# Attention with two shared pairs of PSUM banks, and key preparation in one step with the low parts made by TensorE and ScalarE

## The chip, the cores and the metric

The kernel runs on one core of a Trainium2 chip. The metric is the device time in microseconds (us) of one execution. The engines are named as the profile names them: PE (TensorE, matrix products and transposes into PSUM), DVE (VectorE), ACT (ScalarE), POOL (GpSimd) and SP (SyncE, which issues most transfers). PSUM has eight banks of 128 partitions x 512 float32 values.

## What is computed

The reference has three parts, one behind the other:

```
# attention: q, k, v are (4, 8, 576, 64)
scores = (q @ k.T) / 8
scores = where(scores >= max(scores, -1) - tau, scores, -1e9)
attn   = exp(scores - max);  attn = attn / (sum(attn, -1) + 1e-9)
x      = (attn @ v), heads side by side          # 2304 tokens x 512
# first feed-forward part
xn = x / sqrt(mean(x*x) + 1e-6) * rms_g
x  = (silu(xn @ w_gate) * (xn @ w_val)) @ w_out  # 1536 wide
# second feed-forward part
h  = x @ w_in;  out = (h * cos(h)) @ w_out       # 2048 wide
```

## The kernel before

**Precision.** A float32 product is made of "fp32r" products: each operand is split into a high part (`hi`, the value rounded to that form) and a low part (`lo`, what is left), and three products hi x hi, hi x lo and lo x hi are summed in PSUM. So whatever enters a score product needs a hi and a lo part.

**Tiling of the attention.** The work is 16 pairs of heads (two heads of one batch element). A pair has 576 query rows per head, cut into five units: units 0 to 3 hold 128 rows of both heads, unit 4 the last 64 rows of each head. For a pair the kernel loads q, k and v in their natural layout, transposes q and k on PE, and keeps them as hi and lo tiles in SBUF (`qhi`, `qlo` 128 x 512, `khi`, `klo` 128 x 896: the 576 keys with the last 64 of them a second time, and the last 64 queries). This is the **preparation**, three steps for each pair: "b" (512 key columns), "a" (512 query columns) and "c" (384 more key columns, the last queries among them). Each has a step on PE (`prep_pe`, transposes of 128 x 128), one on ACT (`prep_act`, the hi part, for q multiplied by the scale) and one on DVE (`prep_lo`, PSUM value minus hi part).

**A unit of scores.** `s_mm` makes both heads' scores, 576 columns each, in the bank pairs `s0` and `s1`. DVE's `s_max` copies them to SBUF, negated and scaled, with the row minimum (one instruction per head, 144 in all). For units 0 to 3 the factor is the constant 1.0, since q carries the scale, and for unit 4 the column `qscale`. POOL adds the threshold (`s_thr`), ACT takes the exponential (`s_exp`), and DVE multiplies by the mask and sums the rows (`s_mask`, 144). `t_pe` transposes the result on PE in halves of 64 rows into a PSUM tile `pst`, `t_raw` (ACT) copies it out in two halves, `c_pe` and `c_raw` do the last key columns (`psc`). `av` multiplies by v (20 products into `po`), `av_out` (ACT) copies it out, and POOL divides by the row sums (`av_div`), squares and adds for the norm.

**PSUM before.** Scores have `s0` and `s1`, two banks each. `ps_t` is one bank for the preparation, `psc`, the norm's sums and the fillers; `ps_h` two banks for `pst`; `ps_v` one bank for `po`. Each of the three holds one tile at a time. `px_open`, which opens the first sums of the feed-forward part, takes all three.

**Clock fillers.** `warm` makes products of a constant that nobody reads: ten before the first data, and three after each of the first six units of scores (`WARM_S`), each as two instructions in the trace.

**What sets the order.** The whole program is a list of steps, and class `Plan` lays it out before anything is built: each step has an engine, a duration and a place from the table `STEPS`, the steps it comes after, the buffers that it takes and frees. Again and again the planner picks the step that could start first by these figures (a smaller place wins a tie; `SWITCH` is added on PE where the tiling of the array changes by the table `TILING`; steps named in `LOCK` do not overlap), and writes its instructions. Every engine then works through its own list in that order, and waits where data or a buffer is not there. So a new table of durations and places changes the order everywhere, in the feed-forward parts too. These are two parts of some 820 us in which PE makes 384- and 512-column products; the first eight pieces of them (`gv_mm`, `px_mm`) follow the attention directly.

Of the kernel before, what the change touches and what calls it, by code (L numbers as in the profile page):

```python
# [18 lines left out]
P = 128  # L19
# [9 lines left out]
    "xl3": ("SP", 2500, 3512077, 4000),  # L29
    "yl": ("SP", 3000, 4063563, 3000),  # L30
    "oc0": ("ACT", 482, 1205589),
    "none": ("", 0, -131642),
    "load_k": ("SP", 1700, -358397, 5000),
    "load_q": ("SP", 2300, 2983338, 7000),
    "load_v": ("SP", 1700, 8925207, 5000),
    "pb": ("PE", 440, 3173980),
    "pa": ("PE", 440, 4428866),
    "pc": ("PE", 355, 3941429),
    "pb_a": ("ACT", 467, 6657236),
    "pa_a": ("ACT", 580, 7839742),  # L40
    "pc_a": ("ACT", 360, 2523842),
    "pa_l": ("DVE", 658, 2612355),
    "pb_l": ("DVE", 603, 2495294),
    "pc_l": ("DVE", 470, -3198829),
    "s": ("PE", 884, -3471316),
    "s4": ("PE", 790, 8623278),
    "warm": ("PE", 640, 4878694),
    "max": ("DVE", 678, -148277),
    "exp": ("ACT", 668, 9896803),
    "th": ("POOL", 300, 4051053),  # L50
    "mask": ("DVE", 737, 2741949),
    "t": ("PE", 480, 3967233),
    "t4": ("PE", 250, 3540467),
    "raw": ("ACT", 467, 3428201),
    "raw4": ("ACT", 280, 1719867),
    "c0": ("PE", 245, 4792815),
    "c1": ("PE", 465, 402678),
    "c_raw": ("ACT", 264, 8087658),
    "radd": ("POOL", 250, 5843718),
    "rinv": ("DVE", 420, 3365343),  # L60
    "r_out": ("SP", 2100, 143277, 2500),
    "r_in": ("SP", 1700, 8607246, 11000),
    "av0": ("PE", 2214, 5385146),
    "av1": ("PE", 2748, 4772949),
    "avo": ("ACT", 345, 4838887),
    "div": ("POOL", 1391, 4284936),
    "xout": ("SP", 800, 8555192, 2500),
    "sq": ("POOL", 1124, 5898793),
    "x_add": ("POOL", 1389, 4440748),
    "xsum": ("PE", 1085, 4834622),  # L70
    "mean": ("DVE", 110, -2375958),
    "rms": ("POOL", 1520, 7212247),
    "rs_out": ("SP", 2500, 5265071, 2500),
    "x_load": ("SP", 600, 836615, 4500),
    "x_p": ("POOL", 980, -1347804),
    "x_a": ("ACT", 507, 2440769),
    "x_d": ("DVE", 500, 3806148),
# [218 lines left out]
def attention_moe_cos_kernel(  # L296
# [31 lines left out]
    def f(ap):  # L328
        return ap.bitcast(F32)
# [1796 lines left out]
```

## Time and profile before

| what | value |
|---|---|
| time, median of 3 runs | 1127.99 us (1122.11, 1127.99, 1129.1) |
| the profiled execution's own time | 1124.89 us |
| its span, first to last instruction | 1123.1 us |
| busy share: PE, PEld, DVE, ACT, POOL | 97%, 86%, 78%, 62%, 39% |
| mean granted clock of PE | 0.985 of full speed |
| first and last score maximum on DVE | 12.2 and 284.1 us |
| last product of the attention (`po`) | starts at 298.3 us |

The attention takes the first 300 us, the two feed-forward parts the rest. Busy time counts an instruction from its start to its end, and on an engine that overlaps neighbours (PE above all, DVE and ACT by a few tens of ns) the distance from one start to the next says what an instruction really costs. PE's clock has two levels here, 2.4 GHz (granted 1.0) and 1.2 GHz (granted 0.5).

### The profile page before, as it was taken

What the parts mean: (1) busy time and instruction counts of PE and PEld (TensorE: products, weight loads), DVE (VectorE), ACT (ScalarE), POOL (GpSimd) and SP (SyncE); (2) the same over time, 40 slices, a digit from 0 to 9 for tenths busy, and PEclk for the clock granted to TensorE, in tenths of its full rate; (3) what the DMA queues carried; (4) which work ended last, traced back from release to release, by engine and by line L of the source; (5) the groups of instructions that cost most, each with busy time, mean ns of one, the idle gap of its engine ahead of it and who ended that gap; (6) DMA issues with size and microseconds to landing.
All of it is one profiled execution on the core that took longest, in us unless ns stands there. A gap on an engine that the chain in (4) does not pass through costs nothing.

```text
span 1123.1 us, 19997 instructions
## 1 busy us (share of the span) xinstructions
PE 1084.1 (97%) x7296; PEld 965.8 (86%) x7296; DVE 876.7 (78%) x1683; ACT 693.0 (62%) x1332; POOL 439.3 (39%) x445
## 2 busy tenths in 40 slices
PE   8889999989899999999999999999999999999998
PEld 7666766766799999999999999998888888889887
DVE  4899999899679777778776664598889988865665
ACT  3788888888556555455544443477667676666553
POOL 1143443524622456465421531345554555132221
PEclk6899999999999999999999999999999999999999
DMA  4244342422344455634313285534444453084533
GB/s 107 75 112 134 88 126 77 110 66 68 114 133 169 141 209 193 229 142 132 94 57 114 89 274 173 192 117 153 167 159 155 152 180 124 1 274 167 171 120 94
DMA packets 113458, 153.04 MB, mean 136 GB/s; under 512 B 51632, under 2 KB 82128, under 8 KB 113360
## 3 DMA queue, kind: packets, MB, share of 16 engines
q1 hardware_dynamic: 112000, 151.31, 41.8%
q8 instruction: 57, 0.93, 0.3%
q10 hardware_dynamic: 1264, 0.43, 0.1%
q14 instruction: 41, 0.34, 0.1%
q0 software_dynamic: 96, 0.03, 0.0%
HBM read 103.16 MB, written 48.58 MB: 135 GB/s over the span
## 4 chain that ended last, share of the span: by engine, by line
PE 61%; DVE 16%; ACT 7%; POOL 6%; DMA 5%; issue 4%; SPq 0%; POOLq 0%; DVEq 0%; ACTq 0%
PE pc L840 24%; PE po L840 12%; PE px L840 8%; PE po L733 5%; PE s L600 5%; PE pst L695 2%; DVE s L621 2%; DVE e L650 2%; POOL wtmp L1086 2%; ACT et L706 2%; DMA raw<-in_moe_w_val_dram 2%; POOL wtmp L1168 2%; DMA raw<-in_moe_w_out_dram 1%; PE pgv L840 1%; DMA raw<-in_moe_w_in_dram 1%
## 5 line engine op out<-in xcount | busy, mean ns | idle before, releaser
L840 PE MATMUL pc<-xh,w 128*128 128x384 f32 x896 | 257.2, 338 | 0.9 <-DVE r L1441 0.9
L840 PEld LDWEIGHTS pc<-xh,w 128*128 128x128 f32 x896 | 164.6, 188 | 3.4 <-DVE r L1441 1.2
L840 PE MATMUL pc<-xl,w 128*128 128x384 f32 x448 | 151.1, 337 | 0.0
L1086 POOL TENSOR_TENSOR wtmp<-wtmp,raw 128x512 int32<-128x512 int32 x68 | 90.4, 1336 | 121.9 <-issue 28.4
L840 PE MATMUL pc<-th,w 128*128 128x384 f32 x448 | 134.3, 340 | 2.3 <-ACT r L1445 1.7
L1685 POOL TENSOR_TENSOR h<-hh,h 128x384 fp32r<-128x384 f32 x64 | 66.3, 1041 | 118.1 <-ACT h L1673 47.8
L840 PE MATMUL po<-w,h 128*128 128x512 f32 x405 | 110.0, 397 | 0.2 <-DVE w L1124 0.2
L1441 DVE TENSOR_TENSOR r<-r,pc 128x384 f32<-128x384 f32 x96 | 52.5, 551 | 69.4 <-ACT r L1445 50.6
L650 DVE SCALAR_TENSOR_TENSOR e<-s,th,e 128x576 f32<-128x576 f32 x128 | 103.5, 841 | 0.9 <-POOL th L631 0.9
L1782 DVE TENSOR_TENSOR acc<-acc,po 128x512 f32<-128x512 f32 x126 | 84.6, 682 | 23.9 <-PE po L840 23.4
L840 PE MATMUL px<-h,w 128*128 128x384 f32 x516 | 102.5, 338 | 0.0
L640 ACT ACTIVATE e<-s,m 128x576 f32<-128x576 f32 x128 | 95.4, 790 | 7.9 <-DVE s L621 7.9
L621 DVE TENSOR_SCALAR_CACHE_REDUCE s<-s 128x576 f32<-128x576 f32 x128 | 91.9, 752 | 10.2 <-PE s L600 10.0
L1445 ACT COPY r<-pc 128x384 f32<-128x384 f32 x96 | 45.7, 479 | 84.5 <-PE pc L840 84.2
L706 ACT COPY et<-pst 128x512 f32<-128x512 f32 (+1 forms) x160 | 80.2, 550 | 27.3 <-PE pst L695 27.0
L840 PEld LDWEIGHTS px<-h,w 128*128 128x128 f32 x516 | 91.7, 188 | 0.0
L840 PEld LDWEIGHTS pc<-th,w 128*128 128x128 f32 x448 | 82.5, 188 | 8.1 <-ACT r L1445 3.1
L840 PEld LDWEIGHTS po<-w,h 128*128 128x128 f32 x405 | 75.3, 188 | 15.2 <-DVE w L1124 0.6
L840 PEld LDWEIGHTS pc<-xl,w 128*128 128x128 f32 x448 | 84.2, 188 | 2.0
L1456 POOL TENSOR_TENSOR h<-q,h 128x384 fp32r<-128x384 f32 x43 | 44.7, 1046 | 83.9 <-DVE q L1484 52.4
L840 PE MATMUL pc<-tl,w 128*128 128x384 f32 x224 | 75.6, 337 | 0.0
L631 POOL TENSOR_SCALAR th<-m,tau_c 128x4 f32<-128x4 f32 (+1 forms) x48 | 30.6, 638 | 111.0 <-DVE s L621 110.2
(194 smaller groups left out, 2717.3 us busy)
## 6 DMA issues: line engine op xcount, KB each, us to landing
wd<-w SPq DMA_DIRECT2D x67, 512.0 KB
w<-wd SPq DMA_DIRECT2D x53, 512.0 KB
raw<-in_moe_w_out_dram SPq DMA_DIRECT2D x30, 512.0 KB
raw<-in_moe_w_in_dram SPq DMA_DIRECT2D x16, 512.0 KB
raw<-in_moe_w_gate_dram SPq DMA_DIRECT2D x14, 512.0 KB
raw<-in_moe_w_val_dram SPq DMA_DIRECT2D x14, 512.0 KB
wq<-wd SPq DMA_DIRECT2D x14, 512.0 KB
x<-xb SPq DMA_DIRECT2D x16, 288.0 KB
```

The costliest lines, as they stand in the source:

```text
L600: nc.tensor.matmul(un[n]["ps", hd][:, c, 0:288], lhs, kh[bb][r, k0:k0 + 288], start=c not in [d for d, _ in todo[:x]], stop=c not in [d fo ...
L621: nc.vector.tensor_scalar(s.rearrange("p (c n) -> p c n", c=2), un[n].pop(("ps", hd))[:, :, 0:288], qscale[:, 0:1] if n % 5 == 4 else 1.0, ...
L640: nc.scalar.activation(un[n]["e"][:, hd], un[n]["s", hd], AF.Exp, bias=grp[group_of(n)]["m"][:, c], scale=-1.0)
L650: nc.vector.scalar_tensor_tensor(e, un[n].pop(("s", hd)), grp[group_of(n)]["th"][:, ci:ci + 1], e, op0=ALU.is_le, op1=ALU.mult, accum_out= ...
L706: nc.scalar.copy(dst, src)
L733: nc.tensor.matmul(po[64 * hd:64 * hd + 64, :], vn[:, hd, c, :] if c < 4 else vl[:, hd, :], hf[j]["et"][:, hd, c, :] if c < 4 else hf[j][" ...
L840: nc.tensor.matmul(ps, w[a], x[bb], start=first and i == 0, stop=last and i == 2, skip_group_check=more)
L1086: pool.tensor_tensor(tmp[key], tmp[key], raw.pop(key)[:, :, :, 0], op=ADD)
L1441: return add("ra", at(t0 + when - 60), lambda: vec.tensor_tensor(tile_[o], tile_[o], ps[BANK[n]], op=ADD), after=after + [steps[n]], free= ...
L1445: return add("rc", at(t0 + when - 60), lambda: act.copy(new(o), ps[BANK[n]]), after=[steps[n]] + list(after), take=[("r", ("r", k, o))])
L1685: hs2[x] = add("gl", at(t - 60), lambda: pool.tensor_tensor(H[x][1], g_tile[x], f(H[x][0]), op=SUB), after=[y], free=[("qq", x)])
L1782: vec.tensor_tensor(o, o, oacc.pop((c, q)), op=ADD)
```

## The change

- **PSUM.** `ps_t`, `ps_h` and `ps_v` become one pool of two tiles of two banks each (`pair`). The preparation, `pst`, `psc`, `po`, the norm's sums and the first feed-forward sums all take one of these two; `px_open` takes both.
- **Preparation.** Steps "b" and "c" become one step for all 896 key columns, and all transposes of the preparation work on halves of 64 rows. The hi part of the keys is one ACT copy of 896 columns. The lo part is no longer made by DVE: PE adds minus the hi part to the transposed value in PSUM (`prep_sub`, two products of 448 columns), and ACT copies the result out (`prep_left`). For the first pair, and for the queries, DVE still subtracts. The query's ACT step is a copy without the scale.
- **Scale.** `s_max` now multiplies every unit by the column `qscale`.
- **Fillers.** The 18 after the first six units of scores go. Four stand before the first scores (`warm_s`), and the transposes of the first 14 units have small fillers ahead of them (`WARM_T`, 144 instructions of 64 rows in all).
- **Even halves' last columns.** `c_pe` transposes them in halves of 64 rows too.
- **The table.** All places and many durations in `STEPS` are new, so the order is new on every engine. Two conditions of the feed-forward parts change as well: which block frees a weight (`lastw`), and what the first subtraction of inputs waits for (`zs`).

The diff, cut to its core (the table's lines shown are three of some 130):

```diff
-    "pb": ("PE", 440, 3173980),
-    "pa": ("PE", 440, 4428866),
-    "pc": ("PE", 355, 3941429),
+    "pb": ("PE", 480, -1430370),
+    "pb_s": ("PE", 430, 4917697),
+    "pa": ("PE", 285, -19043596),
...
-WARM = (10, 0, 0, 0)
-WARM_S = (3, 3, 3, 3, 3, 3)
+WARM = (10, 4)
+WARM_T = (6, 6, 6, 6, 6, 6, 6, 6, 5, 5, 4, 4, 3, 3)
...
-    ps_t = m1.enter_context(tc.tile_pool(name="ps_t", bufs=1, space=PSUM))
-    ps_h = m1.enter_context(tc.tile_pool(name="ps_h", bufs=1, space=PSUM))
-    ps_v = m1.enter_context(tc.tile_pool(name="ps_v", bufs=1, space=PSUM))
+    minus = ld_p.tile([P, P], F32R, name="minus")
+    ps_h = m1.enter_context(tc.tile_pool(name="ps_h", bufs=2, space=PSUM))
...
+    def pair(name):
+        return ps_h.tile([P, 2, 512], F32, tag="h", name=name)
...
+    HALVES = slice(0, 64), slice(64, P)
+    def halves_t(ps, c0, src, first=True):
+        for half, r in enumerate(HALVES):
+            nc.tensor.matmul(
+                ps[:, half, c0:c0 + 64], src[r], ident[r, r], start=first, stop=True, is_transpose=True, skip_group_check=True,
             )
...
+            srcs = [nat_flat(k4)] + [nat_flat(kn[:, t]) for t in range(4)] + [nat_flat(k4), q4[p % 2]]
+        for i, src in enumerate(srcs):
+            halves_t(ps, 64 * i, src, not i)
...
+        nc.scalar.copy(prep_view(p, kind, 0, *part), prep_ps(p, kind, *part))
+
+    def prep_sub(p, kind):
+        n, hi = 64 * TILES[kind], prep_view(p, kind, 0)
+        for half in range(2):
+            nc.tensor.matmul(
+                pre[p, kind][:, half, 0:n], minus, hi[:, half], start=False, stop=True, skip_group_check=True,
+            )
+
+    def prep_lo(p, kind, *part):
+        nc.vector.tensor_tensor(
+            prep_view(p, kind, 1, *part), prep_ps(p, kind, *part), f(prep_view(p, kind, 0, *part)), op=ALU.subtract
         )
+
+    def prep_left(p, kind):
+        nc.scalar.copy(prep_view(p, kind, 1), prep_ps(p, kind))
...
-            qscale[:, 0:1] if n % 5 == 4 else 1.0, None,
+            qscale[:, 0:1], None,
...
-        ps = ps_h.tile([P, 2, 512], F32, tag="h", name="pst")
+        ps = pair("pst")
+        for _ in range(WARM_T[n] if n < len(WARM_T) else 0):
+            for half, r in enumerate(HALVES):
+                nc.tensor.matmul(ps[:, half, 0:64], ident[r], ident[r, r], start=True, stop=True)
...
+                    if kind in 'b':
+                        x = add("p" + kind + "_s", n, prep_sub, p, kind, after=[x])
+                        x = add("p" + kind + "_m", n, prep_left, p, kind, after=[x], free=[("pre", p, kind)])
+                    else:
+                        x = add("p" + kind + "_l", n, prep_lo, p, kind, after=[x], free=[("pre", p, kind)])
```

How the order moves is shown at three places. A row is one instruction, or `xN` equal ones, in the order of its engine's list: line, operation, written tile, read tiles and shape; numbers behind a tile's name only tell buffers apart.

**PE, the start of the program.** `warm` are fillers, `psb`, `psa`, `psc` the first pair's preparation, `s_...` the scores of units 0 and 1. Before:

```order
L805 MATMUL warm<-ones 128x128 x10
L526 MATMUL psb<-ident,k_175 128x128
L521 MATMUL psb<-ident,kn 128x128 x3
L521 MATMUL psa<-ident,qn 128x128 x4
L521 MATMUL psc<-ident,kn 128x128
L526 MATMUL psc<-ident,k_175 128x128
L541 MATMUL psc<-ident,q_102 128x128
L600 MATMUL s_226<-khi,qhi 128x288
```

With the change:

```order
L817 MATMUL warm<-ones 128x128 x10
L522 MATMUL psb<-ident,k_170 128x64 x2
L522 MATMUL psb<-ident,kn 128x64 x8
L522 MATMUL psb<-ident,k_170 128x64 x2
L522 MATMUL psb<-ident,q_102 128x64 x2
L522 MATMUL psa<-ident,qn 128x64 x8
L825 MATMUL warm<-ones 128x128 x4
L606 MATMUL s_233<-khi,qhi 128x288
```

All transposes of the first pair now stand in two steps ahead of the scores, with four fillers behind them. Behind this piece, units 0 to 3 follow each other with no filler between (before: three fillers after each).

**ACT, one pair in the middle of the attention.** `khi`, `klo`, `qhi` are the preparation, `e` and `el` exponentials, `et` and `ec` copies of transposes, `t` the copy of `po`. Before:

```order
L555 CAST khi<-psb 128x512
L640 ACTIVATE el<-s,m 128x576
L706 COPY et<-pst 128x8x64 x2
L640 ACTIVATE e<-s,m 128x576 x2
L743 COPY t<-po 128x320
L706 COPY et<-pst 128x8x64 x2
L553 ACTIVATE qhi<-psa,qscale 128x512
```

With the change:

```order
L554 CAST khi<-psb 128x2x7x64
L554 CAST qhi<-psa 128x2x4x64
L646 ACTIVATE el<-s,m 128x576
L570 CAST klo<-psb 128x2x7x64
L712 COPY et<-pst 128x8x64 x4
L734 COPY ec<-psc 128x2x2x64
L646 ACTIVATE e<-s,m 128x576 x5
```

Hi and lo part of the keys now stand close together, around the query's copy and one exponential; on DVE's list the two `klo` instructions of a pair are gone and only `qlo` is left.

**PE, the end of the attention.** `pst` and `psc` are the last transposes, `po` the last products with v, `pgv` the first products of the feed-forward part. Before:

```order
L733 MATMUL po<-et,vn 64x256 x8
L733 MATMUL po<-ec,v_101 64x256 x2
L715 MATMUL psc<-ident,e 128x128 x2
L719 MATMUL psc<-swap,el 128x128
L720 MATMUL psc<-ident,el 64x128
L695 MATMUL pst<-ident,el 128x64 x8
L695 MATMUL pst<-ident,e 128x64 x16
L733 MATMUL po<-et,vn 64x320 x8
L733 MATMUL po<-ec,v_101 64x320 x2
L840 MATMUL pgv<-xh,w 128x384
```

With the change, 48 `pgv` stand between the last scores and these, of which the last is the first row here:

```order
L859 MATMUL pgv<-xh,w 128x384
L724 MATMUL psc<-ident,e 128x128 x2
L721 MATMUL psc<-swap,el 128x128
L722 MATMUL psc<-ident,el 64x128
L745 MATMUL po<-et,vn 64x320 x8
L745 MATMUL po<-ec,v_100 64x320 x2
L522 MATMUL pst<-ident,el 128x64 x8
L522 MATMUL pst<-ident,e 128x64 x48
L522 MATMUL psc<-ident,e 128x64 x4
L745 MATMUL po<-et,vn 64x256 x8
L745 MATMUL po<-ec,v_101 64x256 x2
L745 MATMUL po<-et,vn 64x320 x8
```

So 48 products of the feed-forward part have moved ahead of the last transposes, which are now a block.

## Rows read from the trace of the kernel before

**Rows 1.** By stretch: busy us of PE, PEld, DVE, ACT, POOL (instructions), PEclk, DMA.

```profile
30.00:270.00 240.00, 221.13 (x2575) 163.38 (x2575) 225.26 (x598) 196.64 (x375) 89.14 (x100) 0.99 0.36 96
300.00:1123.10 823.10, 810.40 (x4276) 762.45 (x4274) 613.99 (x977) 461.49 (x896) 329.51 (x318) 0.99 0.45 151
```

**Rows 2.** The maxima's line L621: instruction, count, ns min/median/max, first and last start.

```profile
L621 DVE TENSOR_SCALAR_CACHE_REDUCE s<-s x128: 715/752/759, 12.2 to 282.7; 128x576 f32<-128x576 f32 x128
L621 DVE TENSOR_SCALAR_CACHE_REDUCE s<-s,qscale x16: 804/816/820, 27.5 to 284.1; 128x576 f32<-128x576 f32 x16
```

**Rows 3.** Waits from 30 to 270 us: waiter, releaser, us, times, longest.

```profile
PE pst L695 <- ACT et L706: 7.3, 14, 1.3
DVE s L621 <- PE s L600: 7.3, 10, 1.8
DVE qlo L561 <- ACT qhi L553: 3.5, 5, 0.8
```

**Rows 4.** DVE's timeline in one pair: start us, us, instruction, idle before.

```profile
140.44 0.69 DVE L561 SCALAR_TENSOR_TENSOR klo<-psb,khi 128x512 fp32r<-128x512 f32 x1
141.04 0.68 DVE L418 TENSOR_TENSOR w<-wtmp,w 128x512 fp32r<-128x512 f32 x1
...
144.58 0.75 DVE L561 SCALAR_TENSOR_TENSOR qlo<-psa,qscale,qhi 128x512 fp32r<-128x512 f32 x1 [0.67 <-ACT qhi L553]
145.25 0.81 DVE L650 SCALAR_TENSOR_TENSOR el<-s,th,el 128x576 f32<-128x576 f32 x1
...
146.66 0.56 DVE L561 SCALAR_TENSOR_TENSOR klo<-psc,khi 128x384 fp32r<-128x384 f32 x1
147.13 0.75 DVE L621 TENSOR_SCALAR_CACHE_REDUCE s<-s 128x576 f32<-128x576 f32 x1
```

**Rows 5.** PE's timeline from 144 to 146 us: scores of one unit, then transposes.

```profile
144.53 0.39 PE L600 MATMUL s<-khi,qhi 64*128 64x288 f32 x2
145.14 0.31 PE L600 MATMUL s<-klo,qhi 64*128 64x288 f32 x2
145.28 0.30 PE L600 MATMUL s<-khi,qlo 64*128 64x288 f32 x2
145.51 0.33 PE L521 MATMUL psc<-ident,kn 128*128 128x128 f32 x1
```

**Rows 6.** ACT's preparation from 30 to 270 us, by form: busy us, mean ns.

```profile
L553 ACT ACTIVATE qhi<-psa,qscale 128x512 fp32r<-128x512 f32 x15 | 10.7, 711 | 0.5 <-PE psa L521 0.5
L555 ACT CAST khi<-psb 128x512 fp32r<-128x512 f32 x13 | 7.8, 597 | 0.0
L555 ACT CAST khi<-psc 128x384 fp32r<-128x384 f32 x15 | 7.3, 485 | 2.0 <-PE psc L541 2.0
```

**Rows 7.** Busy time by stretch at the start.

```profile
8.00:25.00 17.00, 15.81 (x77) 13.25 (x78) 8.60 (x21) 5.68 (x9) 0.30 (x1) 0.51 0.56 140
25.00:42.00 17.00, 12.73 (x146) 9.85 (x143) 15.24 (x40) 13.50 (x25) 3.46 (x5) 0.99 0.27 69
```

**Rows 8.** PE's timeline at the start: the wait ahead of step "c", two units' first scores, a filler.

```profile
9.10 0.47 PE L521 MATMUL psc<-ident,kn 128*128 128x128 f32 x1 [1.62 <-DVE qlo L561]
...
13.64 0.61 PE L600 MATMUL s<-khi,qhi 64*128 64x288 f32 x1
...
16.03 1.65 PE L805 MATMUL warm<-ones 128*128 128x128 f32 x6
17.61 0.61 PE L600 MATMUL s<-khi,qhi 64*128 64x288 f32 x1
```

**Rows 9.** PE's timeline at the attention's end.

```profile
283.58 0.29 PE L600 MATMUL s<-khi,klo 128*128 128x288 f32 x1
...
293.92 0.71 PE L695 MATMUL pst<-ident,e 64*128 64x64 f32 x16 [0.74 <-ACT et L706]
295.80 2.37 PE L733 MATMUL po<-et,vn 128*64 128x320 f32 x16 [1.17 <-ACT et L706]
...
298.64 0.44 PE L840 MATMUL pgv<-xh,w 128*128 128x384 f32 x1
```

More of the change, by code (lines that the diff above doesn't have):

```diff
@@ L769, in x_sum @@
         ss = sq.pop(b * NP)
[L770 removed]
+        ps = sq["ps", b] = pair("pss")[:, 0]
         for t in range(5):
@@ L802, in warm, with warm_s @@
         one = ones.broadcast_to([P, P])
-        ps = ps_t.tile([P, 512], F32, tag="t", name="warm")
+        ps = pair("warm")[:, 0]
         for i in range(m):
             nc.tensor.matmul(ps[:, 0:P], one, one, start=True, stop=True)
+    def warm_s(m):
+        one = ones.broadcast_to([P, P])
+        ps = ps_s.tile([P, 2, 512], F32, tag="s0", name="warm")
+        for i in range(m):
+            nc.tensor.matmul(ps[:, 0, 0:P], one, one, start=True, stop=True)
     hq, acc, xrs = {}, {}, {}
@@ L899, in px_open @@
     def px_open(c):
-        xacc[c] = [
-            (ps_t if d else ps_v).tile([P, 512], F32, tag="t" if d else "v", name=f"px{d}")[:, 0:TC]
-            for d in range(2)
-        ]
-        two_ = ps_h.tile([P, 2, 512], F32, tag="h", name="px2")
-        xacc[c] += [two_[:, d, 0:TC] for d in range(2)]
+        banks = [pair("px") for _ in range(2)]
+        xacc[c] = [banks[d // 2][:, d % 2, 0:TC] for d in range(KD)]
     def px_mm(n):
@@ L1272, in t_steps @@
             for kk in range(2):
-                zs.append(add("tz", at(t + 1), lambda kk=kk: z_sub(kk), after=ys[c2] + zs + ([s for s in plan.steps if s["kind"] == "silu_"][:2] if c else []), take=[(ztag, ("z", c, n)) for n in range(2)] if not kk else []))
+                first_ = "silu_" if c else "x_load"
+                zs.append(add("tz", at(t + 1), lambda kk=kk: z_sub(kk),
+                    after=ys[c2] + zs + [s for s in plan.steps if s["kind"] == first_ and (c or any(q == "r" for q, _ in s["take"]))][:2 if c else None], take=[(ztag, ("z", c, n)) for n in range(2)] if not kk else []))
             def psub(a, b, o):
@@ L2083, in attention @@
                     for d in range(KD):
-                        pxc[c, d] = add("pxc" + _, t + n + 4, px_out_, 0, c, d, after=[z, opened], take=[("y", ("acc", 3))] * (c == 3 and not d), free=[("px", c, min(d, 2))])
+                        pxc[c, d] = add("pxc" + _, t + n + 4, px_out_, 0, c, d, after=[z, opened], take=[("y", ("acc", 3))] * (c == 3 and not d), free=[("px", c, d // 2 * 2)])
         moe(plan, gm, g3, gvs, x1, x2, x3, y3, pxc[3, 0])
```

388 lines of the change are left out of this document (183 added, 205 removed).

## The prediction

> **What bounds the kernel now.** I read the busy times by stretch first [rows 1]. From 300 us on PE is busy 810.40 of 823.10 us: that part is bound by PE, with 12.7 us of idle time in it, and the change leaves its instructions as they are. From 30 to 270 us DVE is busy 225.26 of 240 us, ACT 196.64 and PE 221.13, and PE's figure is flattering, since its instructions overlap. Next, the maxima's line [rows 2]: the 16 maxima of unit 4 run from 27.5 to 284.1 us, so a pair takes 256.6 / 15 = 17.1 us, in which DVE works 17.1 x 225.26 / 240 = 16.1 us. Then the waits in that stretch [rows 3]: DVE's idle 14.7 us are 7.3 us for scores, 3.5 us for the query's hi part, and crumbs; PE waits 7.3 us for ACT to empty the only pair of banks of the transposes. So the attention is paced by DVE, with PE and ACT close behind. The last maximum is at 284.1 us, and from there PE ends the attention at 298.64 us [rows 9].
>
> **DVE, the term that decides.** What an instruction costs is its distance to the next start [rows 4].
>
> - The low part of the keys leaves DVE: 141.04 - 140.44 = 0.60 us for 512 columns and 147.13 - 146.66 = 0.47 us for 384. It goes for 15 pairs (the first keeps it): 15 x 1.07 = -16.1 us.
> - Every maximum now takes its factor from a column. The same instruction on the same shape takes 752 ns with the constant and 816 ns with the column [rows 2]: 64 ns for each of 128 instructions, +8.2 us. This is the part of the change that is easily overlooked: it gives half of the gain back.
> - The query's low part becomes a plain subtraction. The plain one beside it took 0.68 us where the query's took 0.75 [rows 4]: 15 x -0.07 = -1.1 us.
>
> Sum -9.0 us, 0.6 us for a pair. The bounds of this term: nothing, if the time only turns into waiting, and -16.1 - 1.1 = -17.2 us, if the column cost nothing.
>
> **ACT, what it takes over.** The copies of 512 and 384 key columns take 597 and 485 ns [rows 6], 0.87 ns a column; 896 columns are then 0.93 us (an estimate from these two rows), twice in a pair: 1.86 instead of 1.08 us. Without the scale, the query's copy should fall from 711 ns to the 597 of the same width. Together +0.66 us a pair, 9.9 us in all. ACT's load is 196.64 us in 240 [rows 1], 14.0 us a pair: 14.7 us then, still under DVE's 15.5. I cost it at nothing on the path, covered by DVE's longer list; if the cover goes, ACT's order (hi part, exponential, low part, then a block of copies) makes PE wait for `klo`, and this is rival 2.
>
> **PE.** Added: two products of 448 columns a pair. A 288-column step of the scores takes 145.28 - 145.14 = 0.14 us [rows 5], so two of 448 are about 0.44 us, 15 times 6.6 us. Taken away: a transpose pair in halves replaces a full one. And fewer changes of tiling: the order has 193 changes ahead of the first `pgv` before, 97 with the change. From the last score to a full transpose PE needs 0.23 us, against 0.14 within the scores [rows 5]: 0.09 us for each change, 96 x 0.09 = 8.6 us less PE work. They are slack only, since it is DVE that has no idle time to speak of in this stretch (6%) [rows 1]; were PE the bound there, the sum below would be 8.6 us lower, at 1103 us. The Trainium skill (TensorEngine Tiling (Array Packing), Key Properties) says that a change of tiling mode drains TensorE, which would make every one of them a loss of PE time. The 0.09 us agree with that. The fillers move: 36 instructions went (18 x 2), a group of six at the low clock cost 17.61 - 16.03 = 1.58 us [rows 8], and 144 small ones come. I cost them at nothing after the first 25 us, because PE has the slack; their price at the start is in the next term.
>
> **The start.** From 8 to 25 us the granted clock is half and DVE is busy only 8.60 of 17 us [rows 7]. One unit of scores takes 16.03 - 13.64 = 2.39 us there and its filler 1.58, 3.97 together [rows 8], while the same unit takes 0.89 us at the full clock (145.28 + 0.14 - 144.53 [rows 5]). With the change nothing stands between the units. Even at the low clock PE then needs 2.39 us for a unit, and DVE, with two maxima of 0.82 us [rows 2] and two masks of 0.81 [rows 4], 3.26 us: DVE becomes the bound at once, and three units gain 0.7 us each. The wait of 1.62 us ahead of the third step of the preparation [rows 8] goes, since that step is gone. That is -3.7 us; I take -4, since DVE's instructions start closer than their durations. Bounds: 0, if the moved fillers fill the gaps elsewhere, and -8.4 us, all of DVE's idle time there.
>
> **The end.** From the last score at 283.6 to the first `pgv` at 298.64 us PE waits for ACT, 0.74 and 1.17 us in the two rows shown [rows 9]. With the change 48 `pgv` stand in this stretch and the transposes have two pairs of banks. I take both waits, -1.9 us; the bounds are 0 and these.
>
> **Sum.** 1124.89 - 9 - 4 - 1.9 = 1110.0 us for the profiled execution. Two shared PSUM tiles in place of three separate ones must cost something that no row of before shows; I add 2 us, about a quarter of the 7.3 us that PE now waits for a bank [rows 3]: 1112. The median of the runs is 1127.99, 3.1 us above the profiled execution, and the lowest is 1122.11, so a median may lie a few us higher than the sum: I predict **1113 us**.
>
> **Rivals.**
>
> 1. *DVE's waits go too.* Two pairs of banks serve the transposes, so ACT and PE no longer hold each other up, and the 3.5 + 7.3 us of DVE's waits [rows 3] shrink by two thirds: another -7, 1105 us. For it: 14 waits of PE for ACT at `pst`. Against it: DVE's largest wait is for scores, which the change does not touch.
> 2. *The shared banks eat the gain.* `po` and the keys' tile each hold one of only two pairs, while there were three tiles before. The keys' tile is held for two ACT copies of 0.93 us, PE's subtraction and the ACT work between: some 4 us a pair. Then scores come late, DVE waits, and the pair stays at 17.1 us. Only start and end remain: 1124.89 - 5.9 = 1119 us. For it: PE works in order, so a transpose that waits for a bank holds up the scores behind it.
> 3. *The order of the feed-forward parts gets worse.* The table is new there too. PE's idle time there is 12.7 us of 823.1 now [rows 1], so there is little to win and more to lose. If it doubles, the attention's gain is cancelled: 1124 us.
> 4. *PE stays at half clock, and the kernel is slower.* The full-array fillers between the first scores go, and what takes their place are 64-row products. From 25 to 42 us the clock was up at 0.99 with transposes and scores alone [rows 7], which speaks against. The Trainium skill (TensorE: Matmul & The Clock Gate, Part 4) says that a transpose does not count as activity for the gate; by that rule the clock would stay low where transposes take the place of products. The trace agrees only at the start, where the clock is low in spite of a busy PE. The price: a unit of scores costs 2.39 instead of 0.89 us, 7.5 us more for the five of a pair; on top of PE's 17.1 x 221.13 / 240 = 15.8 us a pair [rows 1] that is 23.3 against DVE's 15.5, so each pair at the low clock loses some 8 us. It decides from 1.6 pairs (12.9 / 8) more at the low clock than before; three pairs more give 1112 + 24 = 1136 us.
> 5. *The low part does not leave the path:* `klo` then comes later than by DVE, through ACT, PE and ACT, and scores wait for it 0.6 us in each pair. That is the lower bound of the first term and falls together with rival 2.
>
> **Chances.** The forecast (1106 to 1117) 0.54, rival 1 0.12, rivals 2 and 5 0.14, rival 3 0.12, rival 4 0.08. A measurement of this kernel tells about 1% from no change: 11.3 us, so faster means under 1116.7. From the forecast 0.47 lies there (its upper end may miss it by a run's offset), with rival 1 0.59. Within 1% are the rest of the forecast, rivals 2 and 5 and most of rival 3: 0.32. Slower 0.09. The range takes in rival 1 with the start's lower bound, 1105 - 4 = 1101, and rivals 2 and 3 up to 1125.
>
> **What would show it.** In the profile of the change: the maxima at 816 ns in all 144 cases; no `klo` on DVE but for the first pair; unit 4's maxima 16.4 us apart; the first one well before 27.5 us; ACT's copies of 896 columns at about 0.93 us; PE idle for scores no more than before; after the attention the same 12 to 13 us of idle PE. The prediction is wrong if the pairs stay at 17 us, which means that banks or ACT took over, if the granted clock has a longer stretch at 0.5 than 17 us at the start, or if PE's idle time behind 300 us grows.

## The result: 1.1% faster, but not where it was predicted

The changed kernel takes 1113.21 us (median of 5 runs, 1111.91 to 1117.17). The kernel before, run beside it, takes 1125.84 us (5 runs, 1122.11 to 1129.1). The ratio is 0.989 with a 95% interval of 0.9858 to 0.9921. The prediction was 1113 us, and 59% for faster by over 1%.

The number agrees and the reasons do not. The forecast took the gain from the attention and nothing from the feed-forward parts. The traces show it the other way round: in the attention the change gains nothing, and the whole difference of the two spans (1123.1 - 1111.4 = 11.7 us) builds up in the feed-forward parts. The next table shows this by the products of the feed-forward parts, 4272 matmuls in both traces: when the n-th of them starts, in each kernel's own order, after minus before.

| n-th product | 1 | 49 | 145 | 301 | 501 | 901 | 1701 | 2501 | 3301 | last |
|---|---|---|---|---|---|---|---|---|---|---|
| before, us | 298.6 | 307.1 | 324.0 | 355.4 | 391.9 | 465.0 | 608.0 | 753.8 | 920.3 | 1118.4 |
| after - before, us | -12.1 | +0.6 | +3.6 | -0.3 | -0.6 | -2.9 | -4.5 | -7.2 | -11.3 | -11.7 |

The -12.1 at the first product is the 48 gate products that now stand ahead of the attention's end. At the 301st nothing of it is left: -0.3 us. The other 11.4 us come behind it, a little in nearly every stretch.

### The profile page after: what moved, and what is told of

The parts are those of the page before. It is cut to its first block, busy times and chain, and to the rows that moved or that the text cites. A ratio compares the mean times of both kernels' runs of the same rounds, so it can differ in the third digit from the quotient of the medians.

```text
span 1111.4 us, 20987 instructions
## 1 busy us (share of the span) xinstructions
PE 1078.6 (97%) x7794; PEld 976.9 (88%) x7794; DVE 853.1 (77%) x1653; ACT 701.8 (63%) x1333; POOL 438.5 (39%) x445
## 4 chain that ended last, share of the span: by engine, by line
PE 60%; POOL 1%; ACT 0%; DVE 0%; issue 0%; POOLq 0%; ACTq 0%
PE pc L859 32%; PE po L859 18%; PE px L859 10%; POOL wtmp L1183 0%; ACT w L1135 0%; POOL h L1473 0%; POOL h L1702 0%; ACT r L1462 0%; DVE acc L1799 0%; ACT hh L1673 0%; ACT r L1749 0%; DVE q L1501 0%; DVE r L1458 0%; DVE a L1141 0%; DVE q L1495 0%
## 5 line engine op out<-in xcount | busy, mean ns | idle before, releaser
L627 DVE TENSOR_SCALAR_CACHE_REDUCE s<-s,qscale 128x576 f32<-128x576 f32 x144 | 112.8, 813 | 29.4 <-PE s L606 29.1
L712 ACT COPY et<-pst 128x512 f32<-128x512 f32 (+1 forms) x160 | 77.0, 561 | 24.7 <-PE pst L522 24.3
L745 PE MATMUL po<-et,vn 128*64 128x320 f32 (+1 forms) x512 | 68.3, 409 | 2.2 <-ACT et L712 1.9
```

Source lines behind the costliest of these rows:

```text
L627: nc.vector.tensor_scalar(s.rearrange("p (c n) -> p c n", c=2), un[n].pop(("ps", hd))[:, :, 0:288], qscale[:, 0:1], None, op0=ALU.mult, op ...
L712: nc.scalar.copy(dst, src)
L745: nc.tensor.matmul(po[64 * hd:64 * hd + 64, :], vn[:, hd, c, :] if c < 4 else vl[:, hd, :], hf[j]["et"][:, hd, c, :] if c < 4 else hf[j][" ...
```

## The profile after

**The attention.** Busy time by stretch, as in [rows 1], now of the changed kernel:

```profile
30.00:270.00 240.00, 221.85 (x2990) 174.40 (x2990) 212.08 (x559) 201.46 (x369) 92.61 (x101) 0.98 0.36 97
300.00:1111.40 811.40, 802.76 (x4302) 757.06 (x4298) 597.90 (x974) 463.83 (x902) 326.66 (x318) 1.00 0.45 153
```

DVE's busy time from 30 to 270 us fell from 225.26 to 212.08 us, 13.2 us less, more than the 9.0 us that the first term of the prediction asked for. The time did not follow. The maxima's line, as in [rows 2]:

```profile
L627 DVE TENSOR_SCALAR_CACHE_REDUCE s<-s,qscale x144: 775/814/819, 10.2 to 287.4; 128x576 f32<-128x576 f32 x144
```

All 144 have the longer form, as forecast, the first one 2 us earlier (10.2, before 12.2) and the last one 3.3 us later (287.4, before 284.1). Where DVE's time went is in the waits from 30 to 270 us, as in [rows 3] (who waits for whom: us, times, longest):

```profile
DVE s L627 <- PE s L606: 22.8, 31, 2.2
```

```profile
PE s L606 <- DVE s L627: 7.7, 27, 0.4
PE psb L560 <- ACT khi L554: 4.6, 11, 0.8
PE psc L522 <- ACT et L712: 1.4, 2, 0.7
PE po L745 <- ACT et L712: 1.3, 2, 0.7
```

DVE waits 22.8 us for scores, where it was 7.3. The work that DVE lost became waiting. PE's waits for one of the shared banks did shrink: no kind of them takes more than 1.4 us, where `pst` alone had 7.3. Its waits for the scores' own banks, which DVE's maxima empty, did not: 7.7 us in 27 waits, where before had

```profile
PE s L600 <- DVE s L621: 6.0, 13, 1.1
```

And `psb L560 <- ACT khi` is new: 4.6 us in which the subtraction by TensorE waits for ACT's hi part, with the scores of the next unit behind it in PE's list. One such place, first PE, then DVE (start us, us, idle before):

```profile
154.65 0.67 PE L560 MATMUL psb<-khi,minus 128*128 128x448 f32 x2 [0.83 <-ACT khi L554]
155.25 0.40 PE L606 MATMUL s<-khi,qhi 64*128 64x288 f32 x2
...
157.97 0.40 PE L606 MATMUL s<-khi,qhi 64*128 64x288 f32 x1 [0.34 <-DVE s L627]
...
159.61 1.95 PE L745 MATMUL po<-et,vn 128*64 128x256 f32 x16 [0.26 <-ACT ec L734]
...
166.77 0.40 PE L606 MATMUL s<-khi,qhi 64*128 64x288 f32 x2
```

```profile
156.35 0.82 DVE L627 TENSOR_SCALAR_CACHE_REDUCE s<-s,qscale 128x576 f32<-128x576 f32 x1 [0.54 <-PE s L606]
...
166.96 0.81 DVE L656 SCALAR_TENSOR_TENSOR e<-s,th,e 128x576 f32<-128x576 f32 x1
```

At 154.65 PE had waited 0.83 us for `khi`, so the scores came late and DVE waited 0.54 us for them. At 157.97 it is the other way round: PE waits 0.34 us until DVE's maximum has emptied `s`. From 159.61 on PE works seven microseconds at the products with the values, and DVE has little but masks, the last of which starts at 166.96. Two lists, each in a fixed order, wait for each other in turn.

**ACT's preparation** has the sizes that were forecast from [rows 6]: 0.92 us for a copy of 896 columns (forecast 0.93) and 602 ns for the query's (forecast 597).

```profile
L570 ACT CAST klo<-psb 128x896 fp32r<-128x896 f32 x14 | 12.9, 924 | 0.4 <-PE psb L560 0.3
...
L554 ACT CAST qhi<-psa 128x512 fp32r<-128x512 f32 x14 | 8.4, 602 | 0.0
```

**The start,** as in [rows 7], and one place behind it, where the new fillers (`L697`) stand ahead of the transposes:

```profile
8.00:25.00 17.00, 15.01 (x122) 13.27 (x120) 12.40 (x32) 8.72 (x14) 1.72 (x3) 0.70 0.48 109
25.00:42.00 17.00, 15.00 (x207) 13.07 (x208) 13.57 (x36) 11.96 (x20) 2.05 (x4) 0.80 0.57 140
```

```profile
38.91 1.52 PE L697 MATMUL pst<-ident 64*128 64x64 f32 x24
40.25 0.68 PE L522 MATMUL pst<-ident,e 64*128 64x64 f32 x16
```

DVE is busier up to 25 us (12.40, before 8.60) and less busy behind it (13.57, before 15.24): what the scores gain at the start is given back. A full group of fillers (`WARM_T` = 6, which is 24 instructions in the trace) takes 40.25 - 38.91 = 1.34 us at the full clock. `WARM_T` adds up to 12 such groups, 288 instructions and 16 us of PE.

**The end,** as in [rows 9], first one more wait of before, then after:

```profile
289.18 0.71 PE L695 MATMUL pst<-ident,e 64*128 64x64 f32 x16 [0.80 <-ACT et L706]
```

```profile
286.41 0.29 PE L606 MATMUL s<-khi,klo 128*128 128x288 f32 x1
286.54 0.34 PE L859 MATMUL pgv<-xh,w 128*128 128x384 f32 x1
...
294.87 0.38 PE L724 MATMUL psc<-ident,e 128*128 128x128 f32 x2
...
300.72 0.71 PE L522 MATMUL pst<-ident,e 64*128 64x64 f32 x16 [0.51 <-ACT et L712]
301.70 0.34 PE L522 MATMUL psc<-ident,e 64*128 64x64 f32 x4 [0.27 <-ACT et L712]
302.68 1.95 PE L745 MATMUL po<-et,vn 128*64 128x256 f32 x16 [0.64 <-ACT et L712]
...
307.68 0.44 PE L859 MATMUL pgv<-xh,w 128*128 128x384 f32 x1
```

From the last score to the feed-forward part it takes 307.68 - 286.41 = 21.3 us, of which 294.87 - 286.54 = 8.3 us are the 48 products moved in: 12.9 us, where it was 298.64 - 283.58 = 15.1. The term (-1.9) has the size that was forecast, -2.1, and only a part of its reason: the forecast let PE's waits for ACT go, but they fell from 0.80 + 0.74 + 1.17 = 2.7 us to 0.51 + 0.27 + 0.64 = 1.4. The other 0.8 us are work of PE's that now stands ahead of the last score.

**The feed-forward parts.** PE's waits from 350 to 1110 us, first before, then after:

```profile
PE pc L840 <- ACT r L1445: 4.8, 7, 1.9
PE pc L840 <- ACT r L1732: 1.5, 3, 0.8
PE pc L840 <- DVE r L1441: 0.9, 1, 0.9
PE po L840 <- DVE w L1124: 0.2, 1, 0.2
```

```profile
PE pc L859 <- ACT r L1462: 0.7, 2, 0.4
PE pc L859 <- ACT r L1749: 0.7, 1, 0.7
PE po L859 <- POOL h L1702: 0.2, 1, 0.2
```

Before, PE waits 7.4 us, most of it for ACT's copy `r <- pc`, which empties a bank of products; after, 1.6 us. That is only what shows as idle: a wait shorter than the tail of the product before it does not. So I also add up PE's distances from start to start behind 350 us, less those of an undisturbed product (177 ns, and 234 for `po`). What is left over is 10.9 us before and -0.5 us after (a few shorter products make both sums some 4 us too low). The difference, 11.4 us, is the gain. The largest single wait, before, on PE and on ACT:

```profile
639.53 0.61 PE L840 MATMUL pc<-th,a 128*128 128x384 f32 x1 [1.95 <-ACT r L1445]
```

```profile
638.48 0.62 ACT L1120 CAST w<-wtmp 128x512 fp32r<-128x512 f32 x1 [4.54 <-POOL wtmp L1168]
639.00 0.47 ACT L1445 COPY r<-pc 128x384 f32<-128x384 f32 x1
639.37 0.62 ACT L1120 CAST w<-wtmp 128x512 fp32r<-128x512 f32 x1
```

ACT waited 4.54 us at a weight's cast (`w <- wtmp`) for POOL, and the copy that PE needed stood behind that cast: PE lost 1.95 us, and its clock fell right after (from 636 to 646 us 0.83 was granted). The same stretch of the changed kernel, ACT again:

```profile
628.68 0.48 ACT L1462 COPY r<-pc 128x384 f32<-128x384 f32 x1 [1.50 <-PE pc L859]
```

Here it is ACT that waits for PE, and PE for nothing: all of it is busy from 623 to 633 us.

## The experiments

A pair's time is the distance from the first maximum of a pair to that of the next (the prediction read unit 4's maxima); pairs are counted from 0. The mean from pair 4 to pair 15 is 16.69 us before and 16.76 after. PE's clock falls at the start and now and then later, which costs a pair a microsecond or more: pair 11 of the changed kernel takes 16.92 us with a low clock, and 15.81 without, in a kernel below that has the same attention. At an equal clock the change is therefore worth 0.03 us a pair. Kernels with the changed kernel's attention agree within 0.03 us in each later pair without a low clock, so the differences below are means over those pairs from pair 4 on in which neither kernel shows one.

The kernels ran in three series beside the kernel before, whose medians were 1124.76, 1125.56 and 1125.93 us. The intervals of the ratios are some 3 us to either side, so a few us between the medians of two kernels are not shown by the times alone.

### Is it the order of the feed-forward parts?

In the table `STEPS` a kind of step has a duration and a place, here called its preference. These kernels take the attention of one kernel and the feed-forward entries of the other's table:

```diff
+LATE = { ...the feed-forward entries of the other kernel's table... }
...
             out.append(s)
+            if s["kind"] == "av1" and not any(x["kind"] == "av1" and "t" not in x for x in steps):
+                for x in steps:
+                    if "t" not in x and x["kind"] in LATE:
+                        eng_, x["ns"], place, x["landing"] = (LATE[x["kind"]] + (SIGNAL[x["eng"]],))[:4]
+                        x["place"] = place + x["at"] * UNIT
```

The conditions on `tz` and `lastw` were exchanged as well; with either table they move no step in the planner's list of any engine.

**Attention of before, order of after.**

> The kernel before, unchanged up to the last product of probabilities and values; from there the steps of the feed-forward part are put in the order that the changed kernel's table gives them (and its two conditions on tz and lastw, which by themselves move no instruction). The attention's instructions and their order are those of before. Theory A (the gain is the attention's, as predicted): the time stays that of the kernel before, ratio 1.00, some 1126 us. Theory F (the gain is the order of the feed-forward part): PE's lost time behind the attention shrinks from 13.4 us to about 4 to 5, and the time falls by 8 to 12 us, ratio 0.990 to 0.993; the last maximum stays at 284 us.

Measured: 1137.6 us, ratio 1.0111 (1.009 to 1.0132). Neither theory said slower. The trace shows one wait at the hand-over:

```profile
PE pc L940 <- DVE hh L967: 22.4, 1, 22.4
```

While PE waits, ACT waits 2.5 and 4.0 us for transfers of weights. That the new table asks for weights in an order that this attention had not prepared is my reading of it. Against before, the 301st product starts 27.7 us later and the last one 18.2 us later: behind the wait the new order still gains 9.5 us. (The profiled execution is the slowest of the six. 5.5 us of the 27.7 are there at the first product already, in the same instructions: a group of six fillers still takes 1.65 us at 26.9 us, where before takes 0.93 at 25.7, so the clock was low for longer.)

**Attention of after, order of before.**

> The changed kernel, its attention with the 48 early gate products unchanged up to the last product of probabilities and values; from there the steps of the feed-forward part follow the table of the kernel before. Theory A: the gain stays, some 1113 to 1115 us, ratio 0.989. Theory F: the gain goes, 1123 to 1128 us, ratio 0.997 to 1.002, and PE's idle time behind 300 us is back at 12 to 13 us. If both parts carry some of it, this run and the one before each show a half, ratios near 0.995.

Measured: 1131.06 us, ratio 1.007 (1.0043 to 1.0097). The gain is gone, as theory F says, and more: 7.9 us are lost at the hand-over (from +0.5 us at the 49th to +8.5 at the 145th product), and from the 301st (+5.6) to the last (+5.9) nothing is gained. Both runs say the same of the stretch behind 355 us, and both are spoiled by a seam at the attention's end. So the seam was moved to the last `pxc_` step, some 350 us into the run:

```diff
-            if s["kind"] == "av1" and not any(x["kind"] == "av1" and "t" not in x for x in steps):
+            if s["kind"] == "pxc_" and not any(x["kind"] == "pxc_" and "t" not in x for x in steps):
```

> As the first run, but the new table takes over later: the kernel before is unchanged until the eight early units of the first layer are done (its last pxc_ step, about 360 us), and only the rest of the feed-forward part is ordered by the new table. That leaves out the hand-over in which the first run lost one wait of 22.6 us. Theory F (the order of the feed-forward part carries the gain): from that first run's marks, 9.5 us less behind the 300th product, so 1115 to 1118 us, ratio 0.991 to 0.994, PE's lost time behind 360 us at 3 to 7 us against 10 to 11 before. Theory A (the attention carries it): ratio 1.00.

Measured: 1120.27 us, ratio 0.996 (0.9936 to 0.9985). About two fifths of the gain (0.4 of 1.1%); its profiled execution gains 6.3 us, all of it behind the 501st product, with 3.6 us left over in PE's distances behind 350 us (before 10.9). The expected 0.991 to 0.994 was too much: between 735 and 755 us the mixed plan makes new waits of PE (1.70, 1.11 and 0.57 us). Why it makes them is open.

> The changed kernel unchanged until the eight early units are done (about 350 us), the rest ordered by the table of the kernel before. Theory F: 0.6 us ahead of the kernel before at the 500th product and no more at the end, 1122 to 1126 us, ratio 0.998 to 1.002. Theory A: ratio 0.989 as the changed kernel.

Measured: 1123.63 us, ratio 0.9987 (0.9966 to 1.0007). This is the experiment that decides. Up to about 350 us this kernel is the changed one, instruction by instruction; behind it only the order differs, and 1.0% of 1.1% is gone. PE has 9.0 us left over in its distances again and waits as before:

```profile
PE pc L959 <- ACT r L1560: 4.3, 9, 1.9
PE pc L959 <- ACT r L1847: 2.8, 5, 1.0
```

**Durations or preferences?** The durations of before are the bare distances from start to start (`rc` 376 ns, `whi` 521; in the rows above 639.37 - 639.00 = 0.37 us and 639.00 - 638.48 = 0.52 us). The new ones are longer (470 and 590). The next kernel is as the last one, the changed kernel until 350 us, but only `x["ns"]` is replaced:

```diff
-                        eng_, x["ns"], place, x["landing"] = (LATE[x["kind"]] + (SIGNAL[x["eng"]],))[:4]
-                        x["place"] = place + x["at"] * UNIT
+                        x["ns"] = LATE[x["kind"]][1]
```

> The changed kernel, where from the same point on only the planner's durations are those of the table before (silu 375 instead of 420, rc 376 instead of 470, wm 571 instead of 650, and so on); the preferences (place) stay those of the changed kernel. If the gain comes from the longer durations, with which the planner hands PE its operands with more room, it goes: 1120 to 1125 us, ratio 0.995 to 1.000, and PE has some 30 to 40 lost times behind 350 us again. If it comes from the preferences, it stays: ratio 0.988 to 0.991 with some 8 lost times.

Measured: 1129.4 us, ratio 1.0044 (1.0021 to 1.0067), with 15.5 us left over in PE's distances. With the old durations the new preferences are worse than the old table as a whole. So the durations matter; but the two parts of the table belong together, and no run has the longer durations with the old preferences.

By the n-th product, each against before (us):

| n-th product | 49 | 301 | 501 | 901 | 1701 | 2501 | 3301 | last |
|---|---|---|---|---|---|---|---|---|
| after | +0.6 | -0.3 | -0.6 | -2.9 | -4.5 | -7.2 | -11.3 | -11.7 |
| new attention, old order from 350 us | +3.1 | +0.7 | +0.1 | -0.7 | -0.8 | -1.7 | -0.8 | -1.1 |
| the same, old durations only | +1.8 | -0.4 | -0.7 | -1.3 | -1.5 | -0.5 | -0.1 | +4.2 |
| old attention, new order from 360 us | +0.6 | +1.0 | +1.7 | -0.6 | -2.1 | -2.2 | -5.8 | -6.3 |

### What the parts of the attention's change are worth

All of these are the changed kernel with every instruction in its place but those of the edit. First one part undone, the keys' low part back on DVE:

```diff
 def prep_sub(p, kind):
-    for half in range(2):
-        nc.tensor.matmul(pre[p, kind][:, half, 0:n], minus, hi[:, half], start=False, ...)
+    pass
...
 def prep_left(p, kind):
-    nc.scalar.copy(prep_view(p, kind, 1), prep_ps(p, kind))
+    prep_lo(p, kind)
```

> The changed kernel with the keys' low part of the 15 later pairs back on DVE: one subtraction of 896 columns stands in DVE's list where ACT's copy stood, and TensorE's two products are gone; everything else in its place. By the prediction (DVE paces the attention) each costs about 1.07 us: 16 us longer, 1127 to 1130 us, ratio 1.003. If DVE does not pace the attention, since it waits 22.8 us of 240 for scores, the time changes by -3 to +4 us: ratio 0.986 to 0.993.

Measured: 1132.25 us, ratio 1.0068 (1.0044 to 1.0092), 19 us slower than the changed kernel. It looks like the prediction's 16 us, but not all of it is DVE's time. The subtraction takes 1.08 us; a pair without a low clock gets 0.56 us longer (8 pairs), 8 us for 15. PE's wait for `khi` is gone with the edit, and its wait for the maxima, 7.7 us with the change, has grown:

```profile
PE s L602 <- DVE s L623: 18.1, 44, 0.9
```

The rest goes with the clock. In all nine runs the mean granted clock is 0.973 to 0.979, where the five of the changed kernel have 0.986 to 0.991, so the low clock comes with the edit. From 30 to 270 us:

```profile
30.00:270.00 240.00, 214.54 (x2796) 170.45 (x2794) 212.12 (x541) 180.05 (x333) 86.54 (x96) 0.94 0.35 94
```

0.94 is 2 x 0.06 x 240 = 29 us at the lower level, against 2 x 0.02 x 240 = 10 in the row of after. 19 us more at half speed are up to 9.5 us of time; with the 8 that is 17.5 of the 19. The low part's removal is thus worth about 8 us at an equal clock, half of the 16.1 of the prediction. The price of its way over PE, the wait for `khi` among it, is already taken off in these 8 us, since the edit takes both away.

The column in the maxima, taken back (`tau` is not negative here, so the value is the same; the column is there for the other case):

```diff
-            qscale[:, 0:1], None,
+            -SC, None,
```

> The changed kernel with the maxima's factor as a constant of the same value in place of the column: one operand of 144 DVE instructions, nothing else. Each should take 752 ns as in the kernel before instead of 814, 8 to 9 us less DVE work in the attention. Theory A (DVE paces the attention): 1104 to 1106 us, ratio 0.981, last maximum near 279 us. Theory F (DVE does not pace it any longer): within 2 us of the changed kernel, ratio 0.987 to 0.990, and DVE's wait for scores grows from 22.8 us between 30 and 270 us to about 30.

Measured: 1109.71 us, ratio 0.9875 (0.9852 to 0.9898), 3.5 us less than the changed kernel by the medians and 1.7 by the ratios, whose intervals overlap. The maxima took 752 ns, 8.9 us less DVE work:

```profile
L627 DVE TENSOR_SCALAR_CACHE_REDUCE s<-s x144: 716/752/760, 9.8 to 285.1; 128x576 f32<-128x576 f32 x144
```

The pairs show it clearly: a pair gets 0.26 us shorter where DVE has 9 x 0.062 = 0.56 us less to do. Between the two theories, nearer to F.

The small fillers:

```diff
-WARM_T = (6, 6, 6, 6, 6, 6, 6, 6, 5, 5, 4, 4, 3, 3)
+WARM_T = (0,) * 14
```

> The changed kernel without the small products ahead of the transposes of the first 14 units (WARM_T all zero), every step in its place: 144 products fewer on PE. If they are what makes the second and third pair longer (19.6 and 21.8 us from maximum to maximum), those fall to 17 us and the time by 3 to 7 us, ratio 0.983 to 0.986. If they are what keeps the clock up, the granted clock stays at half in a longer stretch than 7 to 27 us and the time is the same or up to 8 us longer, ratio 0.989 to 0.997.

Measured: 1106.11 us, ratio 0.9839 (0.9817 to 0.9861), 7.1 us less than the changed kernel (5.7 by the ratios). The first maximum of pair 4 is at 79.9 us (after 86.7), and from there the pairs are the same (difference 0.00 us). Of the two long pairs only one fell, pair 1 from 19.5 to 14.6 us; pair 2 stays at 22.0 (after 21.9), of which the low clock below can be a microsecond. So the 5 us that pair 2 takes more than before (16.8) are not the fillers'. The clock without them, with ten products ahead of the first data and four ahead of the first scores left in place:

```profile
8.00:25.00 17.00, 14.10 (x104) 12.01 (x104) 13.95 (x36) 10.29 (x18) 1.91 (x3) 0.80 0.52 118
25.00:42.00 17.00, 12.76 (x192) 10.39 (x192) 15.59 (x42) 14.72 (x27) 3.47 (x5) 1.00 0.63 152
42.00:58.00 16.00, 14.10 (x163) 10.03 (x162) 14.82 (x38) 13.02 (x24) 4.54 (x4) 1.00 0.35 92
60.00:68.00 8.00, 6.82 (x74) 6.01 (x76) 7.00 (x17) 5.54 (x9) 1.42 (x2) 0.58 0.51 116
```

In this execution the low stretch at the start is short (0.80 and 1.00, with the fillers 0.70 and 0.80), but from 60 us on there is another one, after waits of PE of 0.70, 0.55 and 1.18 us between 58 and 62 us. The last kernel below has no fillers either. It shows the second stretch too (0.51 from 60 to 67 us), and at the start its clock was 0.50 from 16 to 33 us and 1.00 from there to 60. So a shorter low stretch at the start is not shown to be the fillers' doing.

### What paces the attention

If not DVE, which engine? One kernel each with less work for PE, ACT and DVE; each leaves out a part of the computation:

```diff
-            todo = [(c, t) for c in range(2) for t in (HH, HL, LH)]
+            todo = [(c, t) for c in range(2) for t in ((HH, HL, LH) if n < 5 else (HH, HL))]
```

> The changed kernel without one of the three products of the scores (low keys times high queries, or its like) from the second pair on: two matmuls of 288 columns fewer for each head and unit, 0.28 us a unit or 1.4 us a pair of PE time, 21 us in all; every other instruction keeps its place. It leaves a part of the scores out. If PE's list paces the attention, a pair falls from 16.75 to about 15.4 us and the time by 18 to 21 us, ratio 0.971 to 0.973. If DVE paces it: less than 0.3 us a pair, ratio 0.985 to 0.989. If neither has slack to give because each waits for the other in turn, about half: 0.7 us a pair, ratio 0.979 to 0.981.

```diff
-        nc.scalar.copy(dst, src)
+        nc.scalar.copy(dst[:, :, 0:2], src[:, :, 0:2])     # from unit 10 on; unit 4 of a pair likewise; dst is one of four fixed tiles
```

> The changed kernel, where from the third pair on ACT copies only half of each block of transposed probabilities (256 of 512 columns; the other half keeps older data): 8 copies of 611 ns a pair become about 370, some 2 us a pair off ACT's list, 28 us in all, nothing else. If ACT's list paces the attention: 1.5 to 2 us a pair, ratio 0.965 to 0.970. If not: less than 0.4 us a pair, ratio 0.984 to 0.989.

```diff
+        m = S if n < 5 else 384
-        e = un[n]["e"][:, hd]
+        e = un[n]["e"][:, hd, 0:m]
```

> The changed kernel, where from the second pair on the mask works on 384 of 576 columns: 135 DVE instructions of about 0.82 us become about 0.55, up to 2.4 us a pair off DVE's list, 36 us in all, nothing else. It leaves a third of the columns unmasked. If DVE's list paces the attention: 2 us or more a pair, ratio 0.960 to 0.965. If it does not: less than 0.4 us a pair, ratio 0.984 to 0.989. If DVE and PE wait for each other in turn: about half, 1.0 to 1.4 us a pair, ratio 0.970 to 0.976.

| edit | work taken from one pair | a pair gets | median, us | ratio to before |
|---|---|---|---|---|
| maxima with a constant (DVE) | 9 x 0.062 = 0.56 us | -0.26 | 1109.71 | 0.9875 (0.9852 to 0.9898) |
| shorter masks (DVE), 0.82 to 0.62 us | 9 x 0.20 = 1.8 us | -0.21 | 1110.12 | 0.9867 (0.9838 to 0.9896) |
| one product of the scores less (PE) | 1.4 us | -0.42 | 1105.0 | 0.984 (0.9799 to 0.988) |
| shorter copies (ACT), 605 to 381 ns | 8 x 0.22 = 1.8 us | -0.03 | 1113.21 | 0.9896 (0.9868 to 0.9925) |

The time of ACT's copies is worth next to nothing. Of PE's a third counts (the ratio lies between "half" and "DVE paces it"). Of DVE's it depends on where: of a maximum, which empties the banks that the next scores need, nearly half counts, of a mask a tenth. The copies empty banks too, but PE hardly waits for those any more: what an instruction hands back counts where another engine waits for it. That reading rests on one edit for each kind of instruction. My half-and-half expectation for the mask was wrong, since I had not asked which of DVE's instructions hands something back to PE. With the shorter masks DVE's busy time from 30 to 270 us falls by 18.9 us (212.08 to 193.16), and its wait for scores grows by 17.2 (22.8 to 40.0):

```profile
DVE s L627 <- PE s L606: 40.0, 43, 3.3
```

### The two edits that helped, together

> The changed kernel with both small edits that made it faster by themselves: the maxima's factor a constant of the same value (1.7 us by itself) and no fillers ahead of the transposes (5.7 us by itself). If they add up: 1103 to 1105 us, ratio 0.982. If the fillers' place was what the constant's gain came from: as without fillers alone, ratio 0.984.

Measured: 1102.3 us, ratio 0.9792 (0.9763 to 0.982): 10.9 us less than the changed kernel, where the two by themselves gave 3.5 and 7.1. By the ratios it is 11.0 against 1.7 and 5.7: they add up within the intervals. This is the fastest version, 2.1% below the kernel before. Its last maximum is at 276.2 us, 7.9 us ahead of before's 284.1, and both traces have 24 us of low clock up to there: this is what the attention's change brings once the column and the fillers are out of it.

## Why the prediction was right in its number and wrong in its steps

- **DVE, -9.0 us: the step that failed first.** The instructions changed as counted, and the sum of DVE's busy time fell by more than that. But I took DVE's time for the attention's time, because DVE had 6% of idle time. At an equal clock 0.56 us of the low part's 1.08 count and 0.26 us of the column's 0.56. Unit 4's maxima, for which I had said 16.4 us, stand (287.4 - 23.5) / 15 = 17.6 us apart, before 17.1; from pair 4 on it is 16.8 in both. "Wrong if the pairs stay at 17 us" has come true.
- **Why nothing is left of it.** By the experiments a pair gains 0.56 and loses 0.26, so nearly 0.3 us must go elsewhere, and where is open. It is not the new wait of PE for `khi`, whose price is in the 0.56 already. That PE waits for the shared banks (rival 2) is not borne out: those waits became fewer. But two tiles and a new table also give another order, and no run gives this attention the three tiles or the old order back. The 5 us of pair 2 are open in the same way.
- **The fillers, "at nothing after the first 25 us".** They cost 7.1 us (5.7 by the ratios), and in the trace they are 288 instructions and not 144. The reason given, that PE has slack, is the same error from the other side: slack of an engine in one stretch is not slack in the place where an instruction is put. Their price on PE, 12 groups of 1.34 us, is 16 us; I had set no bound for it.
- **The start, -4.** The first maximum came 2 us earlier and pair 0 took 18.5 instead of 23.7 us, so this part was there (some of it by the clock, which fell at 14 us and before at 8). Pairs 1 and 2 took 19.5 and 21.9 instead of 17.3 and 16.8 us and gave it back: pair 1 with the fillers in it, pair 2 without them just as well.
- **The end, -1.9.** Measured -2.1, of which the waits are 1.3.
- **The shared banks, +2.** No sign of it as a wait for banks.
- **Rivals 1 and 5.** DVE's wait for the query's hi part did shrink (3.5 to 0.7 us from 30 to 270 us), but its wait for scores, which rival 1 also let go, grew from 7.3 to 22.8. The scores' wait for `klo` by way of PE and ACT (rival 5) did not come: up to 300 us PE waits for it once, 0.9 us.
- **The feed-forward parts, 0: the step that failed the other way.** I read 12.7 us of idle PE as "little to win" and thought only of a worse order. Nearly as much was there to win, 11.4 us. The cause is the order: with the old one in the same place the ratio is 0.9987. In the attention of before the new order brought two fifths of it.
- **The clock (rival 4).** It did not happen. The low stretch at the start was 17 us in the trace of after and 24 in that of before (up to 49 us); other executions of the same starts had 17 to 27 us and 20 to some 30 us, so neither kernel is shown to have the longer one. One reading of mine was wrong: from 25 to 42 us the clock of before was not up "with transposes and scores alone", since two groups of full-array fillers stand there, at 25.69 and 27.26 us. The rule on which I had based it, from the Trainium skill (TensorE: Matmul & The Clock Gate, Part 4), would keep the clock low where transposes take the place of products; without the small fillers it was at 1.00 from 25 to 58 us all the same, with scores and products with the values between the transposes.

In sum: +2.8 us up to the last score instead of -11, then -2.1, -0.9 and -11.4. Two errors of 14 and 12 us with opposite signs made a number that agrees, and that is luck.

## What to carry to other kernels

Where a kernel's order comes from a table, a diff that replaces the table is a change to every stage that it orders: price the idle time of the bound engine in all of them, upwards and downwards, before the instructions of one. An engine that is 94% busy need not pace a stage if it and another one hand buffers to each other; ask for each instruction removed what it hands back and who waits for that. Fillers are work like any other, and worth a run without them.

## What the runs showed of the hardware

- The low clock at the start does not have a fixed length. After, the kernel with the old order from 350 us and the one with the old durations have the same instructions up to there. From 8 to 42 us their granted clocks were 0.75, 0.65 and 0.60, which is 17, 24 and 27 us at the lower of the two levels:

```profile
8.00:42.00 34.00, 30.01 (x329) 26.34 (x328) 25.98 (x65) 20.68 (x33) 3.77 (x6) 0.75 0.53 125
```

```profile
8.00:42.00 34.00, 30.14 (x278) 26.49 (x278) 24.53 (x62) 18.30 (x29) 3.77 (x6) 0.65 0.48 119
```

```profile
8.00:42.00 34.00, 30.98 (x278) 26.98 (x277) 23.98 (x62) 18.32 (x29) 3.77 (x6) 0.60 0.48 116
```

  Their 49th products start 0.6, 3.1 and 1.8 us after before's. The Trainium skill (TensorE: Matmul & The Clock Gate, Part 1) says that the number of slow products at a kernel's start differs between runs of the same kernel; the traces agree, with 17, 24 and 27 us.
- A column in place of a constant costs a DVE instruction of 128x576 elements 62 ns (752 to 814), in all 144 cases, both ways.
- In the kernel before, the wait of PE of 1.95 us at 639.53 us was followed by products of 0.52 us instead of 0.34, at the lower clock, for 3.4 us: this late copy cost more than its wait.
